# Moving marks to GpSimd, cutting copies into pieces and shortening idle work in a fused attention, expert and Mish kernel

## The chip, the cores and the metric

The kernel runs on one core of a Trainium2 chip, as one program. The metric is the device time of one execution in microseconds (us). TensorE (PE) does matrix products and transposes, VectorE (DVE), the scalar engine (ACT) and GpSimd (POOL) work on tiles, SyncE (SP) issues most DMA transfers. The engines run side by side and wait for each other at semaphores.

## The reference

Three stages follow each other; the output of each is the input of the next.

```python
def _attn_ref(q, k, v):                   # B 2, H 8, S 768, D 64
    k_sum = k.reshape(B, H, nb, 32, D).max(axis=3)
    v_sum = v.reshape(B, H, nb, 32, D).mean(axis=3)
    scores_l = scale * q @ k^T            # kept where |i - j| < 16
    scores_s = scale * q @ k_sum^T + log(32)
    a = softmax(concatenate([scores_l_m, scores_s]))
    return a @ concatenate([v, v_sum])

def _moe_ref(x, w_skip, w_gate, w1, w2):  # N 1536, D 512, E 8, F 1024
    do_compute = x @ w_skip > 0
    e_idx = argmax(x @ w_gate); gate = softmax(x @ w_gate)[e_idx]
    y = gate * (maximum(x @ w1[e_idx], 0) @ w2[e_idx])
    return where(do_compute, x + y, x)

def _moe2_ref(x, w_in, w_out):            # 1536 x 512 x 2048 x 512
    h = x @ w_in
    return (h * tanh(log1p(exp(h)))) @ w_out
```

## The kernel before

**Attention.** The 16 pairs of batch and head are handled as 8 units `u` of two heads, each in 3 groups `g`, so 24 steps `i = 3u + g`. The order of the work is written out by hand as a software pipeline: step `i` of the loop (`i` = 4 to 20) issues the value product `av(i-1)`, the transposes `tp(i+1)` and `gate_t(i-2)`, and the score products `qk(i+3)` on TensorE; the softmax's `peak(i+2)` (a maximum, L471, and a subtraction, L472, which makes `pr`) and `norm(i-2)` (L507 to L509) on VectorE; copies out of PSUM on the scalar engine. Steps 21 to 23 (`M` = 21) are written out behind the loop. VectorE works its instructions off in the order of the code, so `peak` stands behind whatever was issued before it. A local window of keys or values is 96 rows, of which 16 at either end belong to the neighbouring windows; 24 summary rows are added behind. GpSimd lays these pieces: `halo_v(u)` copies the window's first 32 rows of a unit from the window before it (L115, shape 32x1408), `spread_sums(u)` copies the summary rows into all twelve windows (24x1536).

**Routing.** While attention still works on the second half of the tokens, the first half (`TB` = 6 tiles of 128 tokens, `TT` = 12 in all) is routed by operations that are issued in between, at `r = i - LAG0` with `LAG0` = 16: `choose_ops` (L575 to L589) finds each token's expert, `rank`, `parity` (L610) and `place` find its place in its expert's list, and `choices` (L625) builds the marks: for each tile a 0/1 matrix `sel` of 128x128 (half 0) and of 128x160 (half 1) that says where `pos` equals the token's place `rkp` or `rkf`. The marks are read by the list products `id_first` (L650), behind `av(M)`. The second half of the tokens follows the same way after attention, on the path, with `idle` products (L446, identity by identity, results unused) laid where TensorE would stand still.

**Experts.** Four pairs of experts. The pair's first rows are done by straight code (L1137, L1144). Behind each pair stand two experts' conditional code, skipped by a branch on the counts:

```python
for e in pair:
    with tc.If(count(e) > TQ):        # L1424
        with tc.If(count(e) < ODD):   # L1425
            next_rows(e, own_xT)
        with tc.If(count(e) > HT):    # L1427
            whole(e, spare_of(e))
```

`next_rows` handles the next 32 rows of an expert, `whole` a further tile of 128. With these inputs expert 1 runs `whole`, expert 2 both, expert 5 `next_rows`, the other five skip. Weights stream in by DMA all through the stage, into buffers that come free as TensorE works.

**Tail and second MLP.** `x_first` loads six chunks of 128 rows of x back from DRAM (L1447), `stir_on` issues products whose results are unused (L1565), `x_turn` transposes a chunk (L1468), `x_halves` splits it into a high part (ACT, L1473) and a low part (DVE, L1474), and then the second MLP runs in three passes of high and low parts (L1265, L1539) to the end.

Of the kernel before, what the change touches and what calls it, by code (L numbers as in the profile page):

```python
# [9 lines left out]
F32 = mybir.dt.float32  # L10
# [4 lines left out]
AF = mybir.ActivationFunctionType  # L15
# [5 lines left out]
P = 128  # L21
# [7 lines left out]
def kernel(  # L29
# [13 lines left out]
    nc = tc.nc  # L43
    B, H, S, D = q.shape
# [4 lines left out]
    TB = S // P  # L49
    HP = H // 2  # L50
    QT = 64
# [62 lines left out]
    def copy_pool(out_, in_):  # L114
        nc.gpsimd.tensor_scalar(out=out_, in0=in_, scalar1=1.0, scalar2=1.0, op0=ALU.mult, op1=ALU.mult)  # L115
# [208 lines left out]
            nc.sync.dma_start(out=vw[HALO:BLK, 0, :, VP - D:VP], in_=rows(0, HALO))  # L324
        nc.sync.dma_start(out=vw[lo:WIN - HALO, NQ - 1, :, VP - D:VP], in_=rows(S - WIN + HALO + lo, WIN - HALO - lo))

    def halo_v(u):
        if u >= NU:
            return
        vw = vws[u % NV]  # L330
        copy_pool(vw[0:BLK, 1:NQ, :, VP - D:VP], vw[QT:WIN, 0:NQ - 1, :, VP - D:VP])

    def spread_sums(u, step=NQ):
        if u >= NU:
# [282 lines left out]
    def place_raw(t0, t1, tk):  # L617
        nc.vector.tensor_reduce(out=rkf[:, t0:t1], in_=tk[:, :, 0:E], axis=AX.X, op=ALU.add)

    def choices(t0, t1, half):  # L620
        for t in range(t0, t1):
            if half == 0:
                sels[t] = win.tile([P, 2 * P + TQ], BF16, name=f"sel{t}")
            part_ = slice(P, 2 * P + TQ) if half else slice(0, P)
            nc.vector.tensor_scalar(out=sels[t][:, part_], in0=pos[:, part_],  # L625
                                    scalar1=(rkf if half else rkp)[:, t:t + 1], scalar2=None, op0=ALU.is_equal)

    mvs = {}
# [234 lines left out]
    for i in range(NG + 1, N - 3):  # L863
# [35 lines left out]
        if g == 0:  # L899
            if u == 2:  # L900
                laid_copy(1)
                spread_sums(2)
            place_k(u + 2)
            edge_k(u + 2)
            turn(u + 2, "q")
            load_qk(u + 4, "q")
            if u == 5:
                halo_v(6)
                spread_sums(6)
        elif g == 1:  # L910
            load_v(u + 2)
            if u != 5:
                halo_v(u + 1)
            else:
                spread_sums(7)
            if u > 1:
                block_k(u + 2)
                place_q(u + 2, 0, (nc.scalar, nc.scalar))
            else:
                place_k(3)  # L920
                edge_k(3)
                turn(3, "q")
            if u in (3, 4):
                sums_lay(u - 1)
        elif g == 2:
            if u == 1:
                block_k(3)
                place_q(3, 0, (nc.scalar, nc.scalar))
            place_q(u + 2, 1, (nc.scalar, nc.scalar))
            if u in (3, 4):  # L930
                laid_copy(u - 1)
            if u in (2, 3, 4):
                spread_sums(u + 1)
            turn(u + 3, "k")
            load_qk(u + 5, "k")
# [18 lines left out]
        if r == 1:  # L954
            first = choose_ops(0, TB)
            run(first, 4)
        elif r == 2:
            run(first, 4)
            rk = rank(0, TB, "tr")
        elif r == 3:  # L960
            tk = parity(0, TB)
            place(0, TB, rk, tk)
            place_raw(0, TB, tk)
            choices(0, 3, 0)
            choices(0, 3, 1)
        elif r == 4:
            choices(3, TB, 0)
            choices(3, TB, 1)
            spread_(0, TB, idp)
    M = N - 3  # L970

# [76 lines left out]
    gate_mm_at(M + 2, 0, xp)  # L1048
    gate_sum(NU - 1, 0, xp)
    t0 = TB  # L1050
    idle(ident, ident, 7, P)
    run(choose_ops(t0, TT), 9)
    rk = rank(t0, TT)
    counts_mm()
    idle(ident, ident, 2, P)
    spread_(t0, TT, idp)
    tk = parity(t0, TT)
    counts()
# [4 lines left out]
    id_lists(t0, TT, 0)  # L1063
    EARLY_COUNTS = 5
    for e in range(3):
        idle(ident, ident, 2, P)
        load_counts((e,), (ENG.PE,))
    count_most()
    run(rest, 9)
# [3 lines left out]
    gate_lists(0, TT, 0)  # L1073
    nc.scalar.copy(card.bitcast(F32)[:, :, 1:2], gtp[:, :, 0:1])
    for e in (E, *range(3, EARLY_COUNTS)):
        idle(ident, ident, 2, P)
        load_counts((e,), (ENG.PE,))
    id_lists(t0, TT, 1)
    for i in range(2):
# [83 lines left out]
    def next_rows(e, xT):  # L1163
        at = HT + e % 2 * TQ
        hp_ = acc_h("hw", HM)
        for kk in range(KD):
            w = raws["w1", e, kk].rearrange("p a b -> p (a b)")
            for j in range(4):
                nc.tensor.matmul(hp_[j * TQ:(j + 1) * TQ], xT[:, kk, at:at + TQ],
                                 w[:, j * HM:(j + 1) * HM], start=(kk == 0), stop=(kk == KD - 1))  # L1170
        hT = drawn(flip(relu(hp_, "yo"), "ht"), "hn", nc.scalar)
        yp = acc_h("hw")
        for c in range(2):
            for j in range(4):
                nc.tensor.matmul(yp[j * TQ:(j + 1) * TQ], hT[:, c, j * TQ:(j + 1) * TQ], raws["w2", e, j][:, c, :],
                                 start=(c == 0), stop=(c == 1))
        close(e // 2, yp, at, TQ)
# [11 lines left out]
    def whole(e, xt):  # L1189
# [7 lines left out]
                nc.tensor.matmul(yp, hT[:, f % 4, :], raws["w2", e, f // 2][:, f % 2, :],  # L1197
                                 start=(f == 0), stop=(f == FE // P - 1))

        xT = drawn(flip(xt, "xt"), "xw", nc.scalar, 1)  # L1200
        ha, hb, yp = acc_h("hw"), acc_h("hw"), acc_y()
        g1(ha, 0, 0, KD)
        ra = relu(ha)
# [247 lines left out]

    def x_first():
        x_loads(holds[0][:, 0:1, :], 0, 0)
        x_loads(holds[0][:, 1:CB, :], 0, 1)
        x_loads(holds[1][:, 0:CB, :], 0, CB)

    x_first()
# [106 lines left out]
        for _ in range(n):  # L1564
            nc.tensor.matmul(stir, wi[0, 0][:, 0, 0, 0:P], wi[0, 0][:, 0, 0, :], start=True, stop=True)  # L1565

    stir_on(15)
    xs[0] = [h_[:, c, :] for h_ in holds for c in range(CB)]
    uu = big(0).rearrange("p a b -> p (a b)")
    dd = big(1).rearrange("p a b -> p (a b)")  # L1570
# [7 lines left out]
    for c, tag in enumerate(("acc4", "acc5", "h")):  # L1578
        pt = x_turn(xs[0][c], tag)
        if c == 0:  # L1580
            stir_on(4)
        x_halves(pt, xts[0], c)
    rest = list(enumerate(("h", "acc2", "acc3"), 3))
    for n in range(NN + LAG):
# [75 lines left out]
```

## Time and profile before

| what | value |
|---|---|
| median of 3 runs | 480.3 us (479.56 to 481.8) |
| profiled execution, its own time | 480.68 us |
| its span, first to last instruction | 479.0 us |
| TensorE busy | 450.0 us, 94% |
| VectorE busy | 328.0 us, 68% |
| scalar engine busy | 265.8 us, 55% |
| GpSimd busy | 77.0 us, 16% |
| mean granted TensorE clock | 0.989 |
| attention / routing / experts / reload of x / second MLP | to about 94 / 106.9 / 189.4 / 202.4 / 479 us |

Busy shares are means over the whole span. What a stage is worth is read from its own rows: for each engine when an instruction began, how long it took, and, in brackets, how long the engine had stood idle before it and what it had waited for.

### The profile page before, as it was taken

Reading aid. Unit: us, or ns where it says so; the run is one execution under the profiler, and the core shown is the slowest. Engines: PE = TensorE matmul, PEld = TensorE weight load, DVE = VectorE, ACT = ScalarE, POOL = GpSimd, SP = SyncE. Lnnn points to the kernel's source line nnn. Section 1 sums busy time; section 2 is a strip of 40 time slices with the busy share of each in tenths; the row PEclk is TensorE's granted clock in tenths of the full one; section 3 lists DMA queues with packets and bytes.
Section 4 is the critical chain, followed back from the end, with each engine's and each line's share of the span. In section 5 each row is a group of like instructions: output and inputs, shape, how many; then the busy total and the mean of one; then the engine's idle time right before and its main releaser. Section 6 shows DMA issues by size and latency. Waiting matters only on the chain.

```text
span 479.0 us, 8841 instructions
## 1 busy us (share of the span) xinstructions
PE 450.0 (94%) x3365; PEld 356.2 (74%) x3365; DVE 328.0 (68%) x643; ACT 265.8 (55%) x385; POOL 77.0 (16%) x123
## 2 busy tenths in 40 slices
PE   8999997887999987799999999999999999999996
PEld 7777775763434322588899898999989898999985
DVE  4578789754828732459888899787888886544434
ACT  3686773221221212169687777767676766767560
POOL 4368953054030421000000000000000000000000
PEclk9999998998999999899999999999999999999999
DMA  8989999757999979406122211212121000120003
GB/s 203 245 220 253 275 335 363 284 200 275 392 408 391 356 274 362 138 1 217 47 60 74 69 65 47 86 44 89 44 88 45 1 1 0 43 90 2 0 1 131
DMA packets 43509, 74.48 MB, mean 155 GB/s; under 512 B 18654, under 2 KB 18654, under 8 KB 43168
## 3 DMA queue, kind: packets, MB, share of 16 engines
q1 hardware_dynamic: 42080, 71.96, 46.1%
q0 software_dynamic: 1376, 1.82, 1.2%
q8 instruction: 32, 0.52, 0.5%
q14 instruction: 21, 0.17, 0.1%
HBM read 68.80 MB, written 7.47 MB: 159 GB/s over the span
## 4 chain that ended last, share of the span: by engine, by line
PE 51%; issue 4%; DVE 4%; ACT 2%; DMA 2%; POOLq 0%; POOL 0%; another core or an unknown queue 0%; SPq 0%; DVEq 0%
PE acc L1539 26%; PE hp L1265 25%; PE ptx L1468 1%; DMA big<-xd 1%; DMA xd<-yo,idl 1%; DVE big L1531 1%; DVE big L1520 1%; DVE xt L1474 0%; DVE big L1508 0%; ACT big L1516 0%; DVE big L1528 0%; ACT big L1512 0%; DVE cv L148 0%; ACT big L1505 0%; DVE wo L126 0%
## 5 line engine op out<-in xcount | busy, mean ns | idle before, releaser
L1265 PE MATMUL hp<-xt,wi 128*128 128x384 f32 x768 | 140.3, 336 | 2.3 <-ACT xt L1473 1.4
L1265 PEld LDWEIGHTS hp<-xt,wi 128*128 128x128 f32 x768 | 134.5, 188 | 5.9 <-ACT xt L1473 1.9
L1539 PE MATMUL acc<-wo,big 128*128 128x512 f32 x576 | 138.2, 392 | 0.0
L1539 PEld LDWEIGHTS acc<-wo,big 128*128 128x128 f32 x576 | 107.2, 188 | 20.9
L1505 ACT ACTIVATE big<-hp 128x384 f32<-128x384 f32 x64 | 31.3, 493 | 65.8 <-PE hp L1265 65.7
L1520 DVE TENSOR_TENSOR big<-big 128x768 f32<-128x768 f32 x32 | 30.6, 957 | 30.9 <-ACT big L1516 30.9
L1508 DVE COPY big<-hp 128x384 f32<-128x384 f32 x64 | 35.6, 556 | 23.0 <-ACT big L1505 22.9
L1516 ACT ACT_TABLE_LOAD x32 | 41.1, 1283 | 0.6
L1505 ACT ACT_TABLE_LOAD x31 | 39.8, 1283 | 0.6
L1531 DVE TENSOR_TENSOR big<-big 128x768 fp32r<-128x768 f32 x32 | 30.7, 959 | 3.4 <-DVE big L1528 0.5
L1516 ACT ACTIVATE big<-big,turn 128x768 f32<-128x768 f32 x32 | 30.0, 939 | 0.4
L1512 ACT ACTIVATE big<-big 128x768 f32<-128x768 f32 x32 | 27.1, 847 | 1.0
L471 DVE TENSOR_REDUCE mx<-sps 128x4 f32<-128x480 f32 x24 | 15.7, 654 | 14.1 <-PE sps L463 14.0
L148 DVE SCALAR_TENSOR_TENSOR cv<-raw,cv 128x512 uint32<-128x512 uint32 x32 | 22.2, 692 | 1.1
L151 DVE SCALAR_TENSOR_TENSOR cv<-raw,cv 128x512 uint32<-128x512 uint32 x32 | 21.9, 684 | 0.3
L1130 ACT ACTIVATE hr<-hp 128x512 f32<-128x512 f32 (+1 forms) x10 | 5.6, 556 | 29.1 <-PE hp L1192 11.7
L485 ACT ACTIVATE pts<-tp 120x512 f32<-120x512 f32 x23 | 13.7, 597 | 13.3 <-PE tp L480 12.2
L1528 DVE CAST big<-big 128x768 fp32r<-128x768 f32 x32 | 18.0, 561 | 3.0
L498 PE MATMUL xp<-vw,pts 120*64 120x65 f32 x384 | 17.4, 232 | 2.8 <-issue 1.6
L389 ACT COPY kw<-ptk 64x384 f32<-64x384 f32 x30 | 15.1, 505 | 6.8 <-PE ptk L401 4.7
L138 ACT ACTIVATE cv<-raw 128x512 f32<-128x512 f32 x23 | 15.1, 656 | 4.9 <-DMA raw<-in_moe_w_out_dram 4.9
L498 PEld LDWEIGHTS xp<-vw,pts 120*64 120x64 f32 x384 | 13.7, 141 | 5.3 <-issue 1.4
(233 smaller groups left out, 613.4 us busy)
## 6 DMA issues: line engine op xcount, KB each, us to landing
wb<-in_moe_w_dram SPq DMA_DIRECT2D x28, 512.0 KB
big<-in_moe_w_dram SPq DMA_DIRECT2D x20, 512.0 KB
raw<-in_moe_w_dram SPq DMA_DIRECT2D x16, 512.0 KB
raw<-in_moe_w_in_dram SPq DMA_DIRECT2D x16, 512.0 KB
raw<-in_moe_w_out_dram SPq DMA_DIRECT2D x16, 512.0 KB
kr<-in_k_dram SPq DMA_DIRECT2D x16, 192.0 KB
qr<-in_q_dram SPq DMA_DIRECT2D x16, 192.0 KB
xd<-xb SPq DMA_DIRECT2D x6, 512.0 KB
```

Of the source, the lines that this page charges most:

```text
L148: nc.vector.scalar_tensor_tensor(out=tu, in0=low, scalar=29, in1=tu, op0=ALU.logical_shift_right, op1=ALU.bitwise_or)
L151: nc.vector.scalar_tensor_tensor(out=tu, in0=high, scalar=0xC0000000, in1=tu, op0=ALU.bitwise_and, op1=ALU.bitwise_or)
L498: nc.tensor.matmul(xv[qs, c, h, :], pt[:, j, qs], vw[:, 4 * g + 2 * c + half, h, VP - D - 1:VP], start=True, stop=True)
L1265: last_up[0] = nc.tensor.matmul(ps_, l(a), r(b_), start=(kk == 0 and n == 0), stop=(kk == KD - 1 and n == 2))
L1505: nc.scalar.activation(out=part(ds[n], half), in_=hps[n, half], func=AF.Sigmoid, scale=-1.0)
L1508: nc.vector.tensor_copy(part(us[n], half), hps.pop((n, half)))
L1512: nc.scalar.activation(out=d, in_=d, func=AF.Arctan)
L1516: nc.scalar.activation(out=d, in_=d, func=AF.Sin, scale=-2.0, bias=turn2)
L1520: nc.vector.tensor_tensor(out=u, in0=u, in1=part(ds[n], half), op=ALU.mult)
L1528: nc.vector.tensor_copy(g_part(n, 0, half), part(us[n], half))
L1531: nc.vector.tensor_tensor(out=g_part(n, 1, half), in0=part(us[n], half), in1=g_part(n, 0, half).bitcast(F32), op=ALU.subtract)
L1539: nc.tensor.matmul(accs[t], g[:, a, t * P:(t + 1) * P], wo[f // 2][:, b_, f % 2, :], start=(n in FIRST and m == 0), stop=(n in LAST and m ...
```

## The change

Five edits. (1) At unit 5 the copies `halo_v(6)`, `spread_sums(6)` and `spread_sums(7)` are issued in three pieces each, over 4 of the 12 windows; `halo_v(7)` stays whole. (2) The first half's 12 marks are issued on GpSimd, all at `r` = 3; before, six stood on VectorE at `r` = 3 and six at `r` = 4. (3) The idle products of the routing have 64 columns instead of 128, and there are nine more of them. (4) In `next_rows` relu, transposes and copies go by halves of 128 columns, in `whole` the copy of the transposed tile goes by halves of 256. (5) In the tail the chunks 1 and 2 of x get a load each (256 KB instead of one of 512 KB), and the stirs go from 15 to 12 and from 4 to 2.

```diff
-    def halo_v(u):
+    def halo_v(u, step=NQ):
         ...
-        copy_pool(vw[0:BLK, 1:NQ, :, VP - D:VP], vw[QT:WIN, 0:NQ - 1, :, VP - D:VP])
+        for t in range(1, NQ, step):
+            e = min(t + step, NQ)
+            copy_pool(vw[0:BLK, t:e, :, VP - D:VP], vw[QT:WIN, t - 1:e - 1, :, VP - D:VP])
...
-    def choices(t0, t1, half):
+    def choices(t0, t1, half, eng=nc.vector):
...
-            nc.vector.tensor_scalar(out=sels[t][:, part_], in0=pos[:, part_],
+            eng.tensor_scalar(out=sels[t][:, part_], in0=pos[:, part_],
                                     scalar1=(rkf if half else rkp)[:, t:t + 1], scalar2=None, op0=ALU.is_equal)
...
             if u == 5:
-                halo_v(6)
-                spread_sums(6)
+                halo_v(6, 4)
+                spread_sums(6, 4)
...
             else:
-                spread_sums(7)
+                spread_sums(7, 4)
...
-            choices(0, 3, 0)
-            choices(0, 3, 1)
+            choices(0, TB, 0, nc.gpsimd)
+            choices(0, TB, 1, nc.gpsimd)
         elif r == 4:
-            choices(3, TB, 0)
-            choices(3, TB, 1)
             spread_(0, TB, idp)
...
-    idle(ident, ident, 7, P)
+    idle(ident, ident, 9, QT)
...
-    idle(ident, ident, 2, P)
+    idle(ident, ident, 3, QT)
...
-        hT = drawn(flip(relu(hp_, "yo"), "ht"), "hn", nc.scalar)
+        hr = mo.tile([P, HM], F32, tag="yo", name="hr")
+        hT = mo.tile([P, 2, P], F32, tag="hn", name="hn")
+        pt = mps.tile([P, 2, P], F32, tag="ht", name="pt", bufs=1)
+        for c in range(2):
+            nc.scalar.activation(out=hr[:, c * P:(c + 1) * P], in_=hp_[:, c * P:(c + 1) * P], func=AF.Relu)
+        for c in range(2):
+            nc.tensor.transpose(out=pt[:, c, :], in_=hr[:, c * P:(c + 1) * P], identity=ident)
+        for c in range(2):
+            nc.scalar.copy(hT[:, c, :], pt[:, c, :])
...
-        xT = drawn(flip(xt, "xt"), "xw", nc.scalar, 1)
+        pt = flip(xt, "xt")
+        xT = mo.tile([P, KD, P], F32, tag="xw", name="xw", bufs=1)
+        for c in range(0, KD, 2):
+            nc.scalar.copy(xT[:, c:c + 2, :], pt[:, c:c + 2, :])
...
-        x_loads(holds[0][:, 1:CB, :], 0, 1)
+        for c in range(1, CB):
+            x_loads(holds[0][:, c:c + 1, :], 0, c)
...
-    stir_on(15)
+    stir_on(12)
...
-            stir_on(4)
+            stir_on(2)
```

The edit from 2 to 3 idle products stands at seven places in the program's order (three of them in a loop of three, and three in another). Lines behind the first edit have other numbers in the changed kernel: L625 becomes L627, L745 becomes L747, L471 becomes L473.

VectorE at the end of attention, before, from the marks of `r` = 3 on:

```order
L625 TENSOR_SCALAR sel_1615<-pos,rkf 128x160
L507 TENSOR_SCALAR dn<-xp 128x4
L508 RECIPROCAL dn<-dn 128x4
L509 TENSOR_TENSOR xb_120<-xp,dn 128x2x128
L471 TENSOR_REDUCE mx<-sps 128x4
L472 TENSOR_TENSOR pr<-sps,mx 128x480
L625 TENSOR_SCALAR sel_1666<-pos,rkp 128x128
```

The same place on VectorE in the changed kernel:

```order
L620 TENSOR_REDUCE rkf<-tk 128x6
L509 TENSOR_SCALAR dn<-xp 128x4
L510 RECIPROCAL dn<-dn 128x4
L511 TENSOR_TENSOR xb_120<-xp,dn 128x2x128
L473 TENSOR_REDUCE mx<-sps 128x4
L474 TENSOR_TENSOR pr<-sps,mx 128x480
L635 TENSOR_TENSOR mv<-ohs,idp 128x96
```

The marks (`sel`) are gone from both sides of `peak`; what remains is the normalisation, `peak` and the spread operation `mv`. GpSimd at the same time, before (`vw` are the value windows, `vst` the summary rows, `kw` the key windows):

```order
L115 TENSOR_SCALAR vw_123<-vw_123 32x22x64
L115 TENSOR_SCALAR vw_123<-vst_154 24x24x64
L115 TENSOR_SCALAR vw_124<-vst_154 24x24x64
L115 TENSOR_SCALAR kw_118<-ks 128x12x24
L115 TENSOR_SCALAR vw_124<-vw_124 32x22x64
L745 TENSOR_SCALAR over<-cntf 128x8 x4
```

GpSimd in the changed kernel, of the marks only the first and the last:

```order
L115 TENSOR_SCALAR vw_123<-vw_123 32x8x64 x2
L115 TENSOR_SCALAR vw_123<-vw_123 32x6x64
L115 TENSOR_SCALAR vw_123<-vst_154 24x8x64 x3
L115 TENSOR_SCALAR vw_124<-vst_154 24x8x64 x3
L115 TENSOR_SCALAR kw_118<-ks 128x12x24
L115 TENSOR_SCALAR vw_124<-vw_124 32x22x64
L627 TENSOR_SCALAR sel_1617<-pos,rkp 128x128
...
L627 TENSOR_SCALAR sel_1627<-pos,rkf 128x160
L747 TENSOR_SCALAR over<-cntf 128x8 x4
```

Three copies have become nine, and the twelve marks stand behind the last value copy. The scalar engine in an expert's conditional code, before (`hp` are the products' results, `pt` the transposed tile):

```order
L1130 ACTIVATE hr<-hp 128x256
L389 COPY hn<-pt 128x256
L1425 UNCONDITIONAL_BRANCH x2
L1427 COMPARE_AND_BRANCH
L389 COPY xw<-pt 128x512
```

And in the changed kernel:

```order
L1175 ACTIVATE hr<-hp 128x128 x2
L1179 COPY hn<-pt 128x128 x2
L1436 UNCONDITIONAL_BRANCH x2
L1438 COMPARE_AND_BRANCH
L1211 COPY xw<-pt 128x256 x2
```

Each of the three operations has become two of half the width; `whole`'s other copies stay as they were.

## Rows read from the trace of the kernel before

**Rows 1.** Stretch, us, busy PE PEld DVE ACT POOL (instructions), clock, DMA share, GB/s.
```profile
202.40:479.00 276.60, 271.06 (x1379) 245.11 (x1379) 199.91 (x319) 189.32 (x228) 0.00 (x0) 1.00 0.16 54
```

**Rows 2.** Same view, end of attention and two stretches of low clock.
```profile
70.50:88.00 17.50, 13.82 (x236) 10.40 (x236) 16.71 (x54) 5.46 (x13) 5.52 (x5) 0.90 1.02 370
76.75:80.10 3.35, 3.35 (x47) 2.90 (x44) 3.21 (x11) 0.99 (x3) 0.90 (x1) 0.50 1.00 337
114.30:117.60 3.30, 3.22 (x4) 1.52 (x5) 2.15 (x4) 0.03 (x1) 2.69 (x3) 0.50 1.00 394
```

**Rows 3.** Timeline of PE: start, us, what, xcount, idle before and releaser.
```profile
69.56 0.30 PE L457 MATMUL sps<-mask,unit 64*64 64x240 bf16 x4
...
72.28 0.30 PE L457 MATMUL sps<-mask,unit 64*64 64x240 bf16 x4
...
76.63 0.39 PE L457 MATMUL sps<-mask,unit 64*64 64x240 bf16 x4 [0.76 <-DVE pr L472]
...
87.57 0.63 PE L498 MATMUL xp<-vw,pts 120*64 120x65 f32 x14 [0.88 <-DVE lgs L542]
```

**Rows 4.** Timeline of DVE, end of attention, and one undisturbed operation at 95.03.
```profile
72.28 0.62 DVE L577 TENSOR_TENSOR ca<-lacc,m 128x48 f32<-128x48 f32 x1
73.00 1.33 DVE L579 TENSOR_TENSOR ca<-ca,desc 128x48 f32<-128x48 f32 x1
...
79.36 1.24 DVE L610 TENSOR_SCALAR tk<-ohs 128x24 f32<-128x24 bf16 x1
...
81.07 0.58 DVE L625 TENSOR_SCALAR sel<-pos,rkp 128x128 bf16<-128x128 bf16 x3
...
95.03 0.21 DVE L579 TENSOR_TENSOR ca<-ca,desc 128x48 f32<-128x48 f32 x1
```

**Rows 5.** Timeline of POOL at the same time.
```profile
71.38 2.91 POOL L115 TENSOR_SCALAR vw<-vst 24x1536 f32<-24x1536 f32 x2
...
79.20 1.36 POOL L115 TENSOR_SCALAR vw<-vw 32x1408 f32<-32x1408 f32 x1 [4.40 <-DMA vw<-in_v_dram]
```

**Rows 6.** POOL by line and form: busy us, mean ns of one, idle before.
```profile
L378 POOL TENSOR_TENSOR vb<-vb 96x128 f32<-96x128 f32 x3 | 1.4, 453 | 0.2
...
L115 POOL TENSOR_SCALAR unit<-ident 128x128 bf16<-128x128 f32 x1 | 0.3, 295 | 0.0
```

**Rows 7.** Timeline of PE, idle products near the routing's end.
```profile
102.74 1.13 PE L446 MATMUL idle<-ident 128*128 128x128 f32 x8 [0.96 <-issue]
```

**Rows 8.** PE's branches at two lines: duration ns min/median/max, first and last start.
```profile
L1424 PEldq COMPARE_BRANCH  x8: 70/344/3107, 108.0 to 189.6; - x8
...
L1425 PEldq COMPARE_BRANCH  x5: 68/174/965, 111.4 to 173.7; - x5
```

**Rows 9.** Timeline of PE and ACT in expert 2's conditional code.
```profile
141.17 0.39 ACT L1130 ACTIVATE hr<-hp 128x256 f32<-128x256 f32 x1 [4.41 <-PE hp L1169]
...
141.61 0.44 PE L1120 MATMUL pt<-ident,hr 128*128 128x128 f32 x2 [0.56 <-ACT hr L1130]
142.14 0.37 ACT L389 COPY hn<-pt 128x256 f32<-128x256 f32 x1 [0.58 <-PE pt L1120]
...
142.57 1.92 PE L1175 MATMUL hp<-wb,hn 128*32 128x512 f32 x16 [0.52 <-issue]
...
145.17 0.59 ACT L389 COPY xw<-pt 128x512 f32<-128x512 f32 x1 [2.65 <-PE pt L1120]
...
145.81 0.70 PE L1192 MATMUL hp<-wb,xw 128*128 128x512 f32 x1 [0.73 <-ACT xw L389]
```

**Rows 10.** Timeline of PE at the end of the experts' stage.
```profile
185.74 0.62 PE L1144 MATMUL yp<-big,hn 128*32 128x512 f32 x1 [0.18 <-DMA big<-in_moe_w_dram]
```

**Rows 11.** Timeline of PE and DVE at the reload of x.
```profile
199.81 1.07 PE L1468 MATMUL ptx<-ident,big 128*128 128x128 f32 x8 [0.30 <-DMA big<-xd]
...
201.09 1.29 DVE L1474 TENSOR_TENSOR xt<-ptx,xt 128x512 fp32r<-128x512 f32 x2 [1.04 <-ACT xt L1473]
...
202.43 1.16 PE L1265 MATMUL hp<-xt,wi 128*128 128x384 f32 x5 [0.39 <-DVE xt L1474]
```

More of the change, by code (lines that the diff above doesn't have):

```diff
@@ L1065 @@
     for e in range(3):
-        idle(ident, ident, 2, P)
+        idle(ident, ident, 3, QT)
         load_counts((e,), (ENG.PE,))
@@ L1075 @@
     for e in (E, *range(3, EARLY_COUNTS)):
-        idle(ident, ident, 2, P)
+        idle(ident, ident, 3, QT)
         load_counts((e,), (ENG.PE,))
```

## The prediction

> **What bounds the kernel now.** I read the table by stage first. From 202.4 us to the end TensorE is busy for 271 of 276.6 us [rows 1]; the diff touches nothing in there, so that stage keeps its length and the question is when it begins. Everything ahead of 202.4 us is a chain of short waits of TensorE, so I then read the three places that the diff touches, each by its timeline.
>
> The first is the end of attention. From 70.5 to 88.0 us VectorE is busy for 16.71 of 17.50 us, TensorE for 13.82 [rows 2]: here VectorE sets the pace. The reader should see it in TensorE's rows: three successive score passes begin at 69.56, 72.28 and 76.63 us, 2.72 and 4.35 us apart, the last held by `pr` (L472), and the value product of group 21 begins at 87.57 us after a wait for VectorE [rows 3]. VectorE's own rows tell why: two operations of 48 numbers per partition took 0.62 and 1.33 us, where the same operation took 0.21 us at 95.03 us, and a third (L610) took 1.24 us [rows 4]. GpSimd's rows stand beside them: two value copies fill 71.38 to 74.29 us, one 79.20 to 80.56 us [rows 5], and the slow operations end at just these ends (73.00+1.33=74.33; 79.36+1.24=80.60). VectorE is held until a GpSimd copy is over. The rest of the load is the 12 marks, four rows like that at 81.07 us, 0.58 us for three [rows 4], 2.3 us in all.
>
> The second place is the experts' stage, with short waits around the conditional passes; the third the reload of x before the second MLP.
>
> **Attention's end.** The first two slow operations lose 0.62+1.33-0.42=1.53 us now. A copy of 1.45 us (half of 2.91 [rows 5]) becomes three of about 0.49, my estimate by division, and a held operation can go on at the next seam. Half of the loss stays, by estimate: -0.75 us, so the score pass of 76.63 begins at about 75.85. At L610 VectorE is then earlier by 0.75 us or more, at 78.6 instead of 79.36, ahead of the copy at 79.20 (this one waits for a load and stays whole): its 1.07 us of loss goes. The marks leave VectorE: 2.3 us. That adds to 4.1 us, more than TensorE can take: two more passes at its own 2.72 us from 75.85 end at 81.3, and the value product of 87.57 would start at 84.0, 3.6 us early. [...] I take **-3.0 us**. Bounds: -3.6 (TensorE's pace), and -1.5: the marks' 2.3 less 0.8 that three of VectorE's operations may wait for marks on GpSimd at one mark each.
>
> What do 12 marks cost GpSimd? No row has one. The nearest are a scalar operation of 128x128 into bf16, 295 ns, as the low end, and a product of 96x128, 453 ns, as the high one [rows 6]. A mark is a scalar operation; I take 0.3 us, so they run from 80.6 (behind the copy) to 84.2 us. Their first reader is the list product L650, behind the value product, at 84.0+0.6 to 85.2 us: just hidden. Behind them on GpSimd stands only `over` (L747), which belongs to the routing and waits for work behind these list products.
>
> The row at 73.00 us shows a VectorE operation with two SBUF inputs held for the whole rest of a GpSimd copy. [...]
>
> **Idle products.** Nine more, of 64 columns instead of 128. In rows, eight passes (four products' worth) of 128 columns took 1.13 us behind a wait of 0.96 us [rows 7]; there two products come on top, four passes of about 0.11 us (1.13 less 0.25 for the modelled end, by eight): +0.44. With 0.2 us ahead of the rank products this is +0.65 us if columns don't matter, -0.2 if the cost halves with them. They also move all code behind them by 36 instructions (nine products of two passes, each pass a weight load and a product). A taken branch on TensorE costs between 0.07 and 3.107 us (L1424), and 0.068 to 0.965 us (L1425) [rows 8]. That the jump's price hangs on where the block lies is my reading of this spread; I take it that expert 1's, 0.965, falls to near the median 0.174, -0.75, and that the largest one, at the end of the pairs, stays. Sum **0**, bounds -0.9 to +0.65.
>
> The two rows of branches show stalls of 0.965 and 3.107 us for jumps of a few hundred instructions. [...]
>
> **Halves in the conditional passes.** In expert 2's rows pass the scalar engine's relu took 0.39 us with TensorE waiting 0.56, its copy 0.37 with TensorE waiting 0.52 [rows 9]. From 0.37 (256 columns) and 0.59 (512) a half of 128 costs some 0.28 us by estimate. Now: relu at 141.17, products at 142.57, 1.40 us. Then: first relu 0.28, its transpose 0.25, first copy 0.28, with gaps about 0.95: **-0.45**. In the `whole` pass the copy of 0.59 us begins at 145.17, behind all four transposes, and holds the first product until 145.81, a wait of 0.73 [rows 9]; half a copy takes 0.37 and may begin two transposes (0.3 us) sooner: -0.5 at best, -0.2 if it still waits for all four. I take -0.45, twice (experts 1 and 2). Expert 5's rows pass gains nothing: the product at 185.74 waits for a weight load [rows 10] and sets when the stage ends. Sum **-1.35**, bounds -0.85 to -1.55.
>
> **Tail.** The transposes of chunks 1 and 2 start together at 199.81 when their one load is in; two VectorE subtractions of 0.65 us each then end ahead of the first full run at 202.43 [rows 11]. In two loads the first chunk is turned and split before the second, so one subtraction leaves the path: **-0.65**. Nothing if both land as late as now; -1.3 if both come sooner. Five stirs fewer only matter if TensorE cools (rivals).
>
> **Sum.** -3.0+0-1.35-0.65=-5.0 us. The profiled execution took 480.68 us: 475.7. The median of three runs, 480.3, is 0.4 lower; I say **475.5 us**. A measurement tells about 0.5% (2.4 us) from no change here: faster is below 477.9, slower above 482.7.
>
> **Rivals.**
> 1. The clock stays high (0.18). With shorter waits TensorE doesn't fall to 0.50 at 114.3 us [rows 2]: half of 3.3 us more, **473.9 us**. For it: each low stretch stands behind a wait that shrinks. Against: expert 1's block still begins with a jump and a wait for its copy, which lose 0.75 and 0.45 us only.
> 2. GpSimd is late with the marks (0.12). At 453 ns [rows 6] and more, 0.5 us, they end at 80.6+6.0=86.6, 1.7 behind their need: **477.2 us**.
> 3. VectorE stays held (0.13): the pieces queue back to back without a seam, and the marks hold VectorE's operations with two SBUF inputs as the copies do. Attention gives only -1.5: **477.0 us**. For it: the rows at 72.28 and 73.00; against: most of VectorE's operations there read PSUM.
> 4. Relief without use (0.12): TensorE's own work or its code blocks set the pace, attention gives 0 and the tail nothing: 480.68-1.35-0.4 for the medians, **478.9 us**, no change. For it: TensorE is at 79% and half clock in that stretch [rows 2].
> 5. The marks are the new bound (0.07), the other side: no row shows a comparison on GpSimd. At 0.78 us each they end at 90.0, which eats the whole sum; at 1.0 us they end at 92.6, 7.6 us behind need: 475.5+7.6=**483 us**, slower. They decide against the change from 0.78 us on.
> 6. The tail cools (0.05): with fewer stirs the first products run at 0.50; half of a stretch like the 3.35 us [rows 2], **477.2 us**.
> My forecast has 0.33. The range of eight in ten leaves out what rival 1 may gain beyond its price, rival 5 and the upper half of rival 4: **473.6 to 479.0 us**; the forecast's own is 474.4 to 476.7. Faster: the forecast, 1, and most of 2, 3 and 6, 0.74; no change: 4 and what 2, 3 and 6 leave, 0.19; slower: 0.07.
>
> **What would show it.** In the trace after: the two `choose` operations below 0.7 us and L610 at 0.2; no mark on VectorE before 90 us; GpSimd's marks near 0.3 us and over before the list products; the value product of group 21 near 84.6. The branch of expert 1 near 0.2 us. TensorE waits below 0.35 us in expert 2's passes. The first product of the second MLP near 197.4 us. A mark above 0.5 us, a long row of VectorE beside the marks, or a third slow clock stretch would prove me wrong.

## The result, and the profile after

The changed kernel takes 486.82 us (median of 8 runs, 483.06 to 493.88), the kernel before 481.49 us (8 runs, 479.56 to 482.7): 5.3 us slower. The ratio is 1.0101, with a 95% interval of 1.0057 to 1.0144. I had said 475.5 us and faster. Ratios leave out executions more than 1.5% above the fastest of their kernel (2 of the 8 here, 2 of 12 in a2 and in c2, 5 of 6 in a1, 8 of 12 in a3, 7 of 12 in b3, none in the other kernels below), while the medians are over all executions.

The spread has grown too: 3 us before, 11 us after. The profiled execution took 488.21 us, its span 486.5 us, against 480.68 and 479.0.

First the part that came out as forecast. VectorE's timeline at the end of attention in the changed kernel (start, duration, line, operation):

```profile
77.45 0.21 DVE L579 TENSOR_TENSOR ca<-lacc,m 128x48 f32<-128x48 f32 x1
77.76 0.43 DVE L581 TENSOR_TENSOR ca<-ca,desc 128x48 f32<-128x48 f32 x1
...
83.52 0.16 DVE L612 TENSOR_SCALAR tk<-ohs 128x24 f32<-128x24 bf16 x1
...
83.98 0.20 DVE L620 TENSOR_REDUCE rkf<-tk 128x6 f32<-128x48 f32 x1
```

The three operations that took 0.62, 1.33 and 1.24 us [rows 4] take 0.21, 0.43 and 0.16. TensorE needs 11.25 us from score pass 20 (77.46 us) to the value product of group 21 (88.71 us); before it was 15.29 (72.28 to 87.57 [rows 3]). That is 4.0 us gained between these two profiles. Then GpSimd's and TensorE's timelines, where the bracket holds the idle time before and what ended it:

```profile
84.23 3.52 POOL L627 TENSOR_SCALAR sel<-pos,rkp 128x128 bf16<-128x128 bf16 x6 [3.24 <-DVE dn L509]
87.73 3.97 POOL L627 TENSOR_SCALAR sel<-pos,rkf 128x160 bf16<-128x160 bf16 x6
```

```profile
90.44 0.18 PE L652 MATMUL lp<-mv,sel 128*128 128x16 bf16 x1 [0.48 <-POOL sel L627]
91.09 0.18 PE L652 MATMUL lp<-mv,sel 128*128 128x16 bf16 x1 [0.47 <-POOL sel L627]
91.75 0.42 PE L652 MATMUL lp<-mv,sel 128*128 128x16 bf16 x7 [0.47 <-POOL sel L627]
```

A mark takes 0.59 us (3.52/6) or 0.66 us (3.97/6), not 0.3. They begin at 84.2 us, because the places they compare with are ready only then (`rkf`, L620; the L509 of the bracket is the operation behind it), and end at 91.7, while the list products are due at 89.3: TensorE waits for three of them, 1.4 us. What follows is in the table by stretches (us, busy time of PE, PEld, DVE, ACT and POOL with instructions, granted clock, DMA share, GB/s):

```profile
92.20:95.60 3.40, 3.40 (x32) 2.62 (x34) 1.76 (x9) 1.17 (x3) 0.00 (x0) 0.50 0.40 154
98.90:113.00 14.10, 12.87 (x158) 11.78 (x157) 8.25 (x50) 3.12 (x10) 7.10 (x17) 0.87 0.58 186
109.20:116.00 6.80, 5.99 (x55) 3.02 (x56) 2.64 (x15) 1.27 (x3) 2.99 (x3) 0.51 0.29 73
205.00:208.40 3.40, 3.14 (x14) 2.87 (x14) 0.69 (x1) 0.90 (x2) 0.00 (x0) 0.52 0.85 295
```

Behind the wait TensorE works at a granted clock of 0.50 for 3.4 us; again at the end of routing and the start of the experts (109.2 to 116.0); and again at the reload of x. Before had a low stretch at 76.75, at 114.30 [rows 2] and behind the last branch; the changed kernel has that last one too (198 to 202 us), and the sum of low time is 17 us instead of 10. TensorE's timeline later on:

```profile
147.58 1.92 PE L1183 MATMUL hp<-wb,hn 128*32 128x512 f32 x16 [0.35 <-ACT hn L1179]
150.60 5.42 PE L1200 MATMUL hp<-wb,xw 128*128 128x512 f32 x12 [0.52 <-ACT xw L1211]
...
191.53 0.62 PE L1144 MATMUL yp<-big,hn 128*32 128x512 f32 x1 [1.32 <-DMA big<-in_moe_w_dram]
...
205.26 1.09 PE L1480 MATMUL ptx<-ident,big 128*128 128x128 f32 x4 [2.69 <-DMA big<-xd]
```

The waits in the conditional passes shrink from 0.52 to 0.35 and from 0.73 to 0.52 [rows 9], and the wait for a weight load at the stage's end grows from 0.18 [rows 10] to 1.32. At the reload TensorE stands still for 2.69 us until x lands; in the profile of before it went from the stirs to the first transposes without a wait. The branches (duration min/median/max in ns):

```profile
L1435 PEldq COMPARE_BRANCH  x8: 70/217/2325, 114.9 to 195.3; - x8
...
L1436 PEldq COMPARE_BRANCH  x5: 67/174/449, 119.1 to 178.5; - x5
```

The longest jump at this line fell from 0.965 [rows 8] to 0.449 us, in the direction of the forecast; whether the edit did it is taken up below.

One thing made the two profiles hard to compare: up to score pass 18 the two programs do the same, and the changed one is already 5.2 us later there (71.9 against 66.7 us). Over the sixteen profiles of this study that moment lies between 66.7 and 73.6 us, whatever the kernel; the profile of before is the earliest of all. Of the 7.5 us between the two spans these 5.2 are the larger part, and the reload of x, from the first stir to the second MLP, is 2.7 us more (11.4 against 8.6). So this pair of profiles can't show what the edits cost; runs that undo them one by one can.

### The profile page after: what moved, and what is told of

The parts are those of the page before. It is cut to its first block, busy times and chain, and to the rows that moved or that the text cites. A ratio compares the mean times of both kernels' runs of the same rounds, so it can differ in the third digit from the quotient of the medians.

```text
span 486.5 us, 8880 instructions
## 1 busy us (share of the span) xinstructions
PE 457.3 (94%) x3378; PEld 361.9 (74%) x3378; DVE 323.9 (67%) x631; ACT 266.0 (55%) x391; POOL 84.4 (17%) x141
## 4 chain that ended last, share of the span: by engine, by line
PE 51%; issue 4%; DVE 4%; DMA 3%; ACT 1%; POOL 0%; POOLq 0%; SPq 0%; another core or an unknown queue 0%; DVEq 0%; ACTq 0%
PE acc L1551 25%; PE hp L1276 24%; PE ptx L1480 1%; DMA x<-xd 1%; DMA xd<-yo,idl 1%; DMA big<-xd 1%; DVE big L1543 1%; DVE big L1532 1%; DVE xt L1486 0%; PE hp L1169 0%; DVE cv L151 0%; DVE big L1520 0%; DVE big L1540 0%; DVE wo L126 0%; DVE ot L1566 0%
## 5 line engine op out<-in xcount | busy, mean ns | idle before, releaser
L1551 PEld LDWEIGHTS acc<-wo,big 128*128 128x128 f32 x576 | 107.2, 188 | 20.9
L473 DVE TENSOR_REDUCE mx<-sps 128x4 f32<-128x480 f32 x24 | 15.7, 654 | 17.7 <-PE sps L465 17.7
L1485 ACT CAST xt<-ptx 128x512 fp32r<-128x512 f32 x12 | 7.0, 583 | 18.2 <-PE ptx L1480 18.2
```

Source lines behind the costliest of these rows:

```text
L1551: nc.tensor.matmul(accs[t], g[:, a, t * P:(t + 1) * P], wo[f // 2][:, b_, f % 2, :], start=(n in FIRST and m == 0), stop=(n in LAST and m ...
```

## The experiments

Three theories went into the first runs. **M**: the marks on GpSimd are the loss. **T**: the shorter tail is. **R**: slow clock stretches come and go, also where the diff touches nothing. From the second group on: **I**, the narrow idle products; later **W**, the weight loads set when the experts' stage ends. In each group all kernels were timed in turns with the kernel before on the same chip; "difference" is that of the two medians. The whole set:

| run | what is in it | median (range), us | difference to before |
|---|---|---|---|
| the change | all edits | 486.82 (483.06 to 493.88) | +5.3 |
| a1 | all, marks on VectorE | 489.21 (481.54 to 495.61) | +6.9 |
| a2 | only the marks moved | 485.06 (481.20 to 489.02) | +2.7 |
| a3 | all, tail of before | 489.55 (481.47 to 492.00) | +7.2 |
| a4 | all, marks and tail of before | 485.97 (482.64 to 489.88) | +3.6 |
| b1 | all, idle products of before | 485.27 (482.37 to 488.98) | +2.6 |
| b2 | only the idle products, 9 and 3 of 64 | 488.66 (483.80 to 490.76) | +6.0 |
| b3 | all, idle products 9 and 3 of 128 | 486.26 (478.73 to 490.48) | +3.6 |
| b4 | all, idle products and marks of before | 482.81 (479.73 to 484.88) | +0.2 |
| c1 | only pieces and halves | 483.08 (479.78 to 486.80) | +0.4 |
| c2 | only the tail | 482.31 (478.39 to 487.90) | -0.4 |
| c3 | only idle products, 9 and 3 of 128 | 482.17 (480.07 to 486.64) | -0.6 |
| c4 | b4 with marks shared | 482.90 (478.39 to 485.01) | +0.2 |
| e1 | only idle products, 7 and 2 of 64 | 485.76 (483.18 to 487.70) | +2.6 |
| e2 | what lost nothing, together | 481.83 (479.33 to 486.11) | -1.4 |

**a1, the marks back on VectorE.** In the changed kernel:

```diff
-            choices(0, TB, 0, nc.gpsimd)
-            choices(0, TB, 1, nc.gpsimd)
+            choices(0, 3, 0)
+            choices(0, 3, 1)
         elif r == 4:
+            choices(3, TB, 0)
+            choices(3, TB, 1)
```

> The changed kernel with the 12 marks back on VectorE, six and six; all other edits stay. Theory M (the marks are the loss: 0.59 and 0.66 us each on GpSimd, the list products wait 1.4 us for them and TensorE then runs 3.3 us at a granted clock of 0.50): the wait and the slow stretch go, VectorE gets its 2.3 us back; sum about 1.5 us less than the changed kernel, near 485. Theory T (the tail is the loss): no change from the changed kernel. Theory R (the loss is in slow clock stretches that come and go, also in code that the diff does not touch): no change, and the spread stays as wide as the changed kernel's, some 7 us.

489.21 us, of six executions between 481.54 and 495.61. M did not show: the kernel got no faster. Its profile, of the slowest of the six, has a stretch of low clock from 97 to 122 us that none of the theories had in view, and it hides whatever the marks do.

**a2, only the marks**, the same edit the other way round, in the kernel before.

> The kernel before with only the marks moved to GpSimd. Theory M: marks start behind the places rkp and rkf, at about 81 us, last 7.5 us, so to 88.5, against a need at 88.2 less what VectorE gains (2.3 us): a wait of 2.5 us, a slow stretch behind it, sum +1 to +2 us, 482 to 483.5. Theories T and R: VectorE's relief shows, 2 us less than before, 479.5.

485.06 us, ratio 1.0055 (1.0022 to 1.0089): M, 1.6 us above its range. The profile has the wait for three marks, and behind it a low clock. TensorE's timeline and the table by stretches, of a2:

```profile
86.52 0.18 PE L650 MATMUL lp<-mv,sel 128*128 128x16 bf16 x1 [0.48 <-POOL sel L625]
87.17 0.18 PE L650 MATMUL lp<-mv,sel 128*128 128x16 bf16 x1 [0.48 <-POOL sel L625]
87.83 0.45 PE L650 MATMUL lp<-mv,sel 128*128 128x16 bf16 x7 [0.47 <-POOL sel L625]
```

```profile
87.00:94.50 7.50, 6.85 (x61) 5.00 (x61) 2.94 (x13) 1.56 (x5) 0.78 (x2) 0.54 0.42 159
```

1.4 us of waiting and 7.5 us at a mean clock of 0.54 undo what VectorE had gained by then: from score pass 20 to the first idle product a2 takes 21.8 us, as before does (95.70 less 73.95, 94.12 less 72.28).

**a3 and a4, the tail of before**, without and with the marks on VectorE: `stir_on(15)`, `stir_on(4)`, one load for chunks 1 and 2.

> The changed kernel with the tail of before: 15 and 4 stirs, one load for chunks 1 and 2. Theory T (with 12 stirs TensorE stands still for 2.7 us before x lands and starts the second MLP at half clock): 2 to 2.5 us less than the changed kernel, 484.5, and a narrower spread. Theories M and R: no change.

> Both undone; what stays are the copies in pieces, the idle products and the halves. Theory M+T: the two add, 3.5 to 4 us less than the changed kernel; against before, the halves' 0.7 us and some of VectorE's stalls are gained and the idle products' 0.65 lost: 480.5 to 481.5, no change from before. Theory R: stays at 485 or above.

489.55 and 485.97 us. T is not borne out, and M+T fails by some 5 us. Both profiles again hold a long stretch of low clock between 96 and 119 us. That made theory I: in these kernels the idle products alone are new in that place.

**b1, the idle products of before; b2, only the new ones; b3, the new number at the old width; b4, the old ones and the marks on VectorE.** The edits for b1 and b3 in the changed kernel (the second also in the other six places):

```diff
-    idle(ident, ident, 9, QT)
-    idle(ident, ident, 3, QT)
+    idle(ident, ident, 7, P)      # b1
+    idle(ident, ident, 2, P)
+    idle(ident, ident, 9, P)      # b3
+    idle(ident, ident, 3, P)
```

> The changed kernel with the idle products of before: 7 and 2 of 128 columns in place of 9 and 3 of 64. Theory I (the narrow idle products are the loss: in three of four profiles with them, TensorE stands at a granted clock of 0.50 from about 97 to 117 us, without a gap in the work, where before stays at 1.00 up to 114): no slow stretch between 95 and 110, 5 us and more less than the changed kernel's median, 481 to 483, and a spread of some 5 us like before's. Theory M (the marks): stays at 486 or above, as the marks are still on GpSimd. Theory R (slow stretches come and go whatever the code): stays bimodal, 481 to 492.

> The kernel before with only the idle products changed, to 9 and 3 of 64 columns. Theory I: the slow stretch of 97 to 117 appears in most executions, 5 to 8 us more than before, 487 to 490, spread 10 us. Theories M and R: within 1 us of before.

> The changed kernel with 9 and 3 idle products, but 128 columns each: the same instructions at the same addresses, only the width differs. Theory I by width: as with the old idle products, 481 to 483, with no slow stretch between 95 and 110. Rival (the number of idle products or the shift of the code by 36 instructions is the loss): as the changed kernel, 486 to 490.

> The changed kernel with the old idle products and the marks on VectorE. Theory I+M: a further 1.5 to 2.5 us less than with the old idle products alone, 479.5 to 481, since neither the wait for the marks nor its slow stretch is there. Theory I alone: same as with the old idle products alone, within 1 us.

b2 confirms I and speaks against R: by themselves, with nothing else changed, the narrow idle products cost 6.0 us by the medians, ratio 1.0084 (1.0051 to 1.0116, 2.5 to 5.6 us). Its executions fall into two sets, five of 483.8 to 485.7 us (mean clock 0.978 to 0.987) and seven of 488.3 to 490.8 (0.963 to 0.977), so the median lies in the upper set; the profile shown below is of the slowest. b1 is 485.27, above I's range and below M's, and as much above before as a2: with the old idle products what is left of the loss is that of the marks. b4, without both, stands at before's time (ratio 0.9989, 0.9962 to 1.0015), so the loss is gone but the gain of I+M isn't there. The two costs don't add: 6.0 and 2.7 us alone, 5.3 us in the change. b3 is unclear by its time, 486.26, with the marks still in it; its profile has no low stretch from 95 to 110 us. So I ran the pair without the marks.

**c3, only 9 and 3 idle products of 128 columns**, in the kernel before, against b2, which differs in the width alone (each is set against the kernel before as timed in its own group).

> The kernel before with 9 and 3 idle products of 128 columns: against the kernel that differs only in their width (64), which took 488.66. Theory I by width: no slow stretch between 95 and 110, +0.5 to +1 us over before for nine more products, less what expert 1's jump gains: 482.5 to 483.5. Rival (number or shift of the code): 487 and more.

482.17 us, ratio 1.0012 (0.9982 to 1.0043): no loss. Here are the two routing stages, each from its first idle product to the experts' first product. First b2's stretch and two groups of its idle products, then the same of c3:

```profile
96.20:115.50 19.30, 18.50 (x156) 17.72 (x155) 8.47 (x50) 3.20 (x10) 7.21 (x17) 0.55 0.42 144
```

```profile
103.30 4.08 PE L446 MATMUL idle<-ident 128*128 128x64 f32 x18
107.54 4.08 PE L446 MATMUL idle<-ident 128*128 128x64 f32 x18
```

```profile
96.40:109.90 13.50, 12.26 (x158) 11.36 (x157) 8.36 (x49) 3.12 (x10) 6.62 (x16) 1.00 0.64 211
```

```profile
102.39 1.58 PE L446 MATMUL idle<-ident 128*128 128x128 f32 x12 [0.16 <-PE idle L446]
104.11 0.91 PE L446 MATMUL idle<-ident 128*128 128x128 f32 x6
105.29 1.57 PE L446 MATMUL idle<-ident 128*128 128x128 f32 x12 [0.27 <-PE idle L446]
```

The same instructions in the same order, 5.8 us apart in these two profiles. With 64 columns the clock falls during the first idle passes, at 98.0 us, and its mean over the stretch is 0.55 of full; 18 passes (nine products of two passes each) take 4.08 us (0.22 each), and TensorE is never done with them in time: no pass waits for anything, its own idle work has become the path. With 128 columns the clock stays at 1.00, 12 passes take 1.58 us (0.13 each, the modelled end included), and TensorE even has short gaps.

Where the clock is full, the width makes next to no difference. The first idle group of the changed kernel, ahead of its low stretch, and that of c3:

```profile
98.89 2.20 PE L448 MATMUL idle<-ident 128*128 128x64 f32 x18
```

```profile
96.44 2.25 PE L446 MATMUL idle<-ident 128*128 128x128 f32 x18
```

So narrowing saved at most 0.05 us in 18 passes, and what it cost is the clock.

**e1, the old number, 7 and 2, at 64 columns.**

> The kernel before with the old number of idle products, 7 and 2, at 64 columns in place of 128. Theory I by width alone: the slow stretch of 97 to 117 us comes in most executions, 486 to 490. Rival (width and number together: fewer products leave the same gaps and TensorE is no busier, so the stretch comes only with 9 and 3): 482 to 484.

485.76 us, ratio 1.0038 (1.0009 to 1.0068), and the closest spread of all, 483.18 to 487.70: every one of its 12 runs had a mean clock of 0.967 to 0.977, while before's, in turns with it, had 0.977 to 0.993, in the middle 0.988. The number lies just below the range of width alone and above that of width and number together. I read it so that both count: the low clock comes with the width, and each product more then costs its longer time. Its stretch, and a group of 12 passes in it (0.23 us each):

```profile
96.40:112.40 16.00, 15.04 (x142) 14.13 (x143) 8.47 (x50) 3.25 (x10) 7.23 (x17) 0.56 0.52 173
```

```profile
105.67 2.80 PE L446 MATMUL idle<-ident 128*128 128x64 f32 x12
```

Over all profiles the time from the first idle product to the experts' first product falls into three sets: 12.8 to 13.5 us with 128 columns (ten kernels), 15.9 with 7 and 2 of 64, and 19.1 to 20.1 with 9 and 3 of 64 (a1, a3, a4, b2); the changed kernel's own profile, with 14.1, is the one where the low stretch came late, at 109 us.

**c1, only pieces and halves; c2, only the tail**, by leaving the other edits out.

> The changed kernel with marks, idle products and tail all as before: only the copies in pieces and the halves are left. My sum as it stood: -0.75 to -1.8 from VectorE's shorter stalls, -1.35 from the halves, 479.5 to 480.5 against 482.5 for before, if it arrives at the end; theory W (the weight loads set when the experts' stage ends, the product that waits for a load at 185.7 us takes it all): no change from before, within 0.7 us.

> The kernel before with only the new tail: loads of 256 KB for chunks 1 and 2, 12 and 2 stirs. Theory T (with fewer stirs TensorE stands still until x lands, and a slow stretch falls on the first products of the second MLP): +1 to +2.5 us, 483.5 to 485. My sum as it stood: -0.65 us. Rival (the slow stretch there comes as often with 15 stirs, since x lands 4.5 to 7 us behind the store): within 0.7 us of before.

483.08 us, ratio 1.001 (0.9979 to 1.004), and 482.31, ratio 0.998 (0.9945 to 1.0015). c1's time is what W said: no change. The gains in the passes are there (waits of 0.36 and 0.52, as in the changed kernel), and TensorE waits longer for a weight load at the stage's end. Its row (the profile is of c1's slowest execution, 486.80 us), and the same row of b2:

```profile
190.35 0.62 PE L1146 MATMUL yp<-big,hn 128*32 128x512 f32 x1 [1.51 <-DMA big<-in_moe_w_dram]
```

```profile
194.89 0.62 PE L1144 MATMUL yp<-big,hn 128*32 128x512 f32 x1 [1.49 <-DMA big<-in_moe_w_dram]
```

From the experts' first product to this one it is 79.4 us in c1 (110.91 to 190.35), in the profile of before 78.8 (106.90 to 185.74). But b2, which has no halves, has 79.4 us too (115.51 to 194.89), and c2, without them as well, 77.5 with a wait of 0.73. So the wait varies by itself, and W is argued, not shown. c2 speaks for its rival: T is gone, and my 0.65 us can't be told from nothing.

**c4, marks shared**: the six of 160 columns on GpSimd, the six of 128 on VectorE, in b4.

```diff
-            if half == 0:
+            if t not in sels:
                 sels[t] = win.tile([P, 2 * P + TQ], BF16, name=f"sel{t}")
...
+            choices(0, TB, 1, nc.gpsimd)
             choices(0, 3, 0)
-            choices(0, 3, 1)
         elif r == 4:
             choices(3, TB, 0)
-            choices(3, TB, 1)
```

> The kernel with old idle products and the marks shared: the six of 160 columns on GpSimd, the six of 128 columns on VectorE. GpSimd takes 6 times 0.66, 4.0 us from the places on (84.1 in the changed kernel, where the list products are due at 89.3): ready in time, so no wait of TensorE and no slow stretch behind it; VectorE has 1.2 us less. Theory M (GpSimd is late because 12 marks take 7.5 us): 1 us less than with all marks on VectorE, 481 to 482. Rival (any mark on GpSimd holds VectorE or TensorE): 484 and more, like the kernels with 12.

482.90 us, ratio 0.9993 (0.9954 to 1.0032). GpSimd's and TensorE's rows:

```profile
85.73 4.24 POOL L627 TENSOR_SCALAR sel<-pos,rkf 128x160 bf16<-128x160 bf16 x6 [3.94 <-DVE rkf L620]
...
91.71 0.70 PE L652 MATMUL lp<-mv,sel 128*128 128x16 bf16 x18
```

The marks end at 90.0, the list products run at 91.7 without a wait. The stage works as M says (18.5 us from score pass 20 to the first idle product, against 21.8 before and 19.9 in b4, which differs in the marks alone), but the time at the end does not move.

**e2, what lost nothing, together**: copies in pieces, shared marks, 9 and 3 idle products of 128, halves, loads of 256 KB, 15 and 4 stirs.

> What lost nothing, put together: copies in pieces, marks shared between GpSimd and VectorE, 9 and 3 idle products of 128 columns, halves, loads of 256 KB with 15 and 4 stirs. If the gains arrive: 3 us from attention's end and 0.7 from the halves, less 0.5 for the idle products, 479 to 480 against 482.5. Theory W (the weight loads of the experts' stage set its end): within 1 us of before, and the wait for a weight load near the stage's end at 1 to 2 us instead of 0.2.

481.83 us, 1.4 below before's median, ratio 0.9991 (0.9953 to 1.0028): not to be told from no change. Its profile has 18.8 us from score pass 20 to the first idle product, 3 us better than the profile of before (the others with before's code there, b2, c2, c3 and e1, have 20.9 to 23.1). The product that W names waits longer than before's 0.18 [rows 10], but less than W asks for:

```profile
176.74 1.92 PE L1138 MATMUL hp<-wb,xT 128*32 128x512 f32 x16 [0.57 <-DMA wb<-in_moe_w_dram]
...
186.92 0.62 PE L1145 MATMUL yp<-big,hn 128*32 128x512 f32 x1 [0.81 <-DMA big<-in_moe_w_dram]
```

c2, with nothing of that gain, has 0.56 and 0.73 us at the same two products, so W is not settled here either. Nor is where the 3 us went: the scatter of the first 72 us, 7 us over the profiles, is larger than they are.

## Why the prediction was wrong

The sum was -5.0 us: -3.0 for attention's end, 0 for the idle products, -1.35 for the halves, -0.65 for the tail. Measured alone, in medians, the marks are +2.7 (a2), the idle products +6.0 (b2), pieces and halves +0.4 (c1), the tail -0.4 (c2).

**The idle products: the step that failed.** I put them at 0, between -0.9 and +0.65 us, by reckoning what the added passes cost in time: "+0.65 us if columns don't matter, -0.2 if the cost halves with them". Both ends took TensorE's clock as given. At full clock columns indeed don't matter (2.20 against 2.25 us for 18 passes), but the clock did not stay: alone the narrow products cost +6.0 us by the medians, 2.5 to 5.6 by the ratio (b2). With 64 columns in place of 128 the clock falls to 0.50 and stays there until after the experts' products have begun (b2: from 98.0 to 118.5 us, their first at 115.51); the small work on the path then takes nearly twice as long (a list product with its two idle passes 0.53 us in b2, 0.28 in c3). I had read the low stretches as what follows a wait [rows 2], and so looked for them behind waits only. That the width does it is shown by b2 against c3, which differ in it alone and the intervals of whose ratios don't meet (1.0051 to 1.0116, 0.9982 to 1.0043), and by e1. Why the clock falls with the narrow passes, and not in every execution of b2, no run here shows.

**The marks: a mis-sized term.** I took 0.3 us each; they took 0.59 and 0.66, 7.5 us for the twelve instead of 3.6. The nearest row, a copy of 128x128 in 0.295 us [rows 6], was half of the 0.59 that a comparison of that size with a number per partition took. I also let the marks start behind GpSimd's last copy, though the places they need come from VectorE's rows; but that made them too late, not too early: 8.3 us behind score pass 20 by the forecast (80.6 against 72.28), 6.8 in the changed kernel (84.23 against 77.46). So the price alone makes them late. Rival 2 had the mechanism but priced it at +1.7 against the forecast; a2 is +2.7 against before. The wait of 1.4 us and the low stretch behind it, which the rival left out, eat the whole gain of attention's end. Where a2's 2.7 us then come from is open; in its profile the experts' stage, from the first product to the first stir, takes 88.2 us against 86.1.

**Attention's end: the size was right, the parts of it only in part.** -3.0 was forecast up to the value product. The 0.6 us by which it stays short of the -3.6 of TensorE's pace was my estimate, and no run shows it as a term; in the changed kernel and in a2 the low clock came behind the value product, 3.4 us at 0.50 and 7.5 us at a mean of 0.54. Between the profiles it is -4.0 for the changed kernel and -4.5 for a2 (15.3 to 10.8 us); but the four other profiles with before's code in that place have 14.4 to 15.9. With the pieces and the marks on VectorE it is 13.4 to 14.3 us (a1, a4, b4, c1), about 1 us less; without the marks on VectorE the pieces add nothing (10.8 in a2, 10.9 to 12.3 in four profiles with them). Part of what the profile of before lost there was chance: the three operations of 0.62, 1.33 and 1.24 us [rows 4] took 1.36, 0.41 and 0.77 in c2 and 0.31, 0.21 and 0.16 in a2, all with the copies whole, as the copies happened to fall. In the changed kernel L612 ran behind the whole copy, which ended at 80.99 us, and not ahead of it as I had said. The row at 73.00 ended with a copy (74.33 against 74.29 us), and rival 3 had the marks hold VectorE in the same way. VectorE's timeline in the changed kernel, beside the marks of 84.2 to 91.7 us:

```profile
86.08 0.39 DVE L635 TENSOR_TENSOR mv<-ohs,idp 128x96 bf16<-128x96 bf16 x1
...
88.38 0.27 DVE L544 TENSOR_TENSOR lgs<-lgs,xp 96x128 f32<-96x128 f32 x1
```

`mv`, with two inputs in SBUF, took 0.39 us against 0.25 before, L544 its usual 0.27: 0.14 us in all. The gain is then given back: by the wait for the marks, by the low stretch behind it, or, with shared marks, somewhere that these runs don't tell.

**The halves: half as large, and not seen at the end.** I said -0.45 for each of three passes; their bound of -1.55 should have been -1.45 (0.45 and twice 0.5). The waits shrank by 0.11 and 0.17 us in the rows pass and by 0.21 in each `whole` pass, 0.7 us in all. c1 is at +0.4, -1.0 to +1.9 by its ratio, so whether they arrive can't be told. That the product which waits for a weight load at the end [rows 10] takes them in is argued, not shown.

**The jump: near the number, but by luck.** 0.965 became 0.449 us, where I had said 0.174; the largest one, 3.107 us, stayed large at 2.325. I had put it down to the shift of the code by 36 instructions. All eight kernels with the shift have 0.421 to 0.449 us, but c2, c4 and e1, without the added idle products, have 0.421 to 0.426 too, while before, a2, b1, b4 and c1 have 0.705 to 1.105. So the jump falls without the shift as well, and what sets its length stays open.

**The tail: neither borne out nor excluded.** c2 is at -0.4, -2.7 to +0.7 by its ratio, and the stirs don't decide it either: b2, with the tail of before, waits 2.29 us for x (at 207.06), as the changed kernel waits 2.69. How late x lands differs more between executions than the edit can move. In the changed kernel's profile the transposes of chunks 1 and 2 still run together, against what I had said the two loads would do.

**The rivals.** Rival 5, the slower one, looked at GpSimd; no rival let the clock fall in routing. The chance of 0.07 for slower came from leaving out a case, more than from a wrong weight of one.

## What to carry to other kernels

Work that is laid in to keep TensorE busy is chosen by the granted clock that the rows show beside it, not by its length: before narrowing it, change the width alone and read the clock over that stage. An operation that moves to another engine is priced by a row of the same kind, with its operands (here a comparison with a number per partition), and is timed from the last of its inputs, not from when the engine is free. A delay that one profile shows is looked for in a second one of the same kernel before its removal is counted as a gain: here the held operations and the jump changed by themselves. And shorter waits enter a sum only when a run with that edit alone shows them at the end.

## What the runs showed of the hardware

A busy TensorE stayed at the low clock in routing: in b2 it was busy for 18.50 of 19.30 us at a mean of 0.55, mostly in back-to-back passes of 64 columns in fp32, and in e1 for 15.04 of 16.00 us at 0.56. With passes of 128 columns in the same place the mean was 1.00 (c3). Not every execution with narrow passes shows it: the changed kernel's profile kept the full clock over its first ones, to 109 us.

GpSimd took 0.587 us for a comparison of 128x128 in bf16 with a number per partition (3.52/6 in the changed kernel), and for 128x160 0.66 us there and 0.71 in c4 (4.24/6); VectorE took about 0.19 us for the mark of 128x128 [rows 4].

What L577, a VectorE operation with two SBUF inputs, took went by where it met a GpSimd copy: 0.21 us in e1 and 0.31, 0.33, 1.09 and 1.36 us in a2, b2, c3 and c2, the last four ending 0.06 us or less behind a copy's end (c2: 76.67 against 76.61).

The program up to score pass 18, the same in all kernels, takes between 66.7 and 73.6 us, from one profile to the next. In the changed kernel's profile eight idle passes at 7.6 us took 2.08 us, where before's took 1.16, both at full clock and with the same waits ahead of them.
